# Program order on three engines in the first 18 slots of a fused attention and channel-mix kernel

## The chip, the cores and the metric

The kernel runs on one core of a Trainium2 chip. The metric is device microseconds of one execution. The core's engines run side by side and meet through semaphores: TensorE (PE in the profile, its weight loads as PEld), VectorE (DVE), ScalarE (ACT), GpSimd (POOL) and SyncE (SP), whose queue issues nearly all the transfers between HBM and the on-chip memory.

## What is computed

Biased attention over 4 batches of 8 heads, 768 positions and 64 channels a head, and behind it a channel mix with 512 channels in and 1024 hidden ones. Cut to what matters:

```python
# attention, per batch and head
scores = q @ k.T / sqrt(64) - slope[h] * dist         # kept: causal and within n_local = 96, or first n_global = 8 columns
a = exp(scores - max) / (sum + 1e-9)
x = a @ v                                             # to (batch, 768, 512)
# channel mix
xk = mu_k * x + (1 - mu_k) * x_prev                   # x_prev: the row before, zeros first
xr = mu_r * x + (1 - mu_r) * x_prev
k = maximum(xk @ w_k, 0)
out = sigmoid(xr @ w_r) * (k * k @ w_v)
```

The three weight matrices arrive as 64-bit floats (read as pairs of 32-bit words), everything else as 32-bit floats; the result is 32-bit.

## The kernel before, in words

The 3072 rows are 24 **tiles** of 128 rows, six a batch. Tiles are the steps of the main loop (line 526), and each step has four **slots**, one for each pair of heads (`hp`), so slot = 4 x step + hp. Two tiles make a **chunk** of the channel mix, 12 in all.

In a slot of an early step (0 to 8) the program traces, in this sequence: the last stage of some weights, the first stage of some weights, `transposes` for the tile of the step before, the middle stage of some weights, `scores` for this tile, `weighted` for the tile before, and then channel-mix work for 2 x 2.5 units (`run_ffn`). `scores` has the score matmuls (line 318 for the first seven tiles, in plain 32-bit; lines 320 and 321 afterwards, in split form), the bias and row maximum on VectorE (line 326) and the exponential on ScalarE (line 327), with, at the end of a tile, the reciprocals of the sums (lines 334 and 335). `transposes` turns the exponentials (line 354) and copies them out of PSUM on ScalarE (line 355). `weighted` multiplies by v (line 379), spreads the reciprocals with small matmuls (line 368), copies these on ScalarE (line 370) and, at the tile's end, forms x on VectorE (line 392).

The **weights** come as 20 blocks of 128 x 512 in four stages: `weight_load` (a 512 KB transfer), `weight_begin` (absolute value of the upper words on ScalarE, line 184, then a scaling on GpSimd, line 185), `weight_bits` (three bit operations on VectorE, lines 195 to 197, and the rounded half by ScalarE or GpSimd in turn, line 198) and `weight_end` (the rest on GpSimd, line 203). `w_pace` says how many blocks each stage should have reached at a slot: the first stage by this slot's count, the bits by that of the slot before, the end by that of two slots before, the loads five ahead. Blocks 0 to 7 are w_k, 8 to 11 w_r, 12 to 19 w_v. Raw blocks 0 to 2 and 11 to 19 lie in a pool of three buffers (`p4k`), which also holds the raw q and k from tile 8 on, the raw q of tile 7 and the mixing results; blocks 3 to 10 borrow the buffers of the first chunk. The working copies lie in a pool of four (`f2`), shared with the squared activations and the sigmoids; the middle results lie in a PSUM pool of three buffers (`ps_f`), shared with all the channel mix's matmul results.

The **channel mix** of a chunk has 40 units: 16 of kp (lines 439 to 441, then relu, square and split in lines 465 to 468 after each four), 8 of z, 16 of vps. Chunk 0 is mixed in two halves by `mix_first`, traced in slots 8 and 11, and its units start with slot 11; chunk 1 joins the queue in slot 19, with a budget of -17.5 units (line 512).

**What sets the order.** The program's trace gives each instruction a priority. A planner then lays out every engine's queue ahead of the run: it simulates a timeline and takes, on each engine, the earliest traced instruction that is ready by its own estimate, so that a queue may hold instructions in another order than traced. `keep_in_program_order` ties an instruction to the one traced before it on its engine, which fixes their sequence in the queue and adds no semaphore. The class `InOrder` wraps an engine so that its instructions are tied while `on` is true. Before the change it wraps SyncE, tied up to the end of slot 0, and ScalarE for the absolute values of blocks 0 to 7 alone. (The wrapped instructions appear under line 44.) TensorE is not wrapped.

At the start GpSimd fills with zeros the lower half of the partitions of two q buffers and two double k buffers (lines 226 and 227), 64 partitions of 1024 and 2048 elements, so that tiles with 64 channels can be multiplied as 128.

Of the kernel before, what the change touches and what calls it, by code (L numbers as in the profile page):

```python
# [9 lines left out]
F32 = mybir.dt.float32  # L10
# [4 lines left out]
AF = mybir.ActivationFunctionType  # L15
# [36 lines left out]
@with_exitstack  # L52
def tile_biased_attention_channel_mix(ctx: ExitStack, tc: tile.TileContext, qT, kT, v, n_sizes, mu_kr, w_k, w_v, w_r, q_rows, k_rows, v_rows, slopes, out):
    nc = tc.nc
    vec, act, pool, pe = nc.vector, nc.scalar, nc.gpsimd, nc.tensor
    act_in_order, sync = InOrder(tc, nc.scalar), InOrder(tc, nc.sync)

    const = ctx.enter_context(tc.tile_pool(name="const", bufs=1))

# [43 lines left out]
    zeros = const.tile([128, 512], BF16, name="zeros")  # L103
# [36 lines left out]
    for h in range(H):  # L140
        c = -8.0 * 2.0 ** -(h + 1)
# [10 lines left out]
    for h in range(H):  # L152
        c = -8.0 * 2.0 ** -(h + 1)
# [10 lines left out]
    w_raw, w_two = {}, []  # L164
# [14 lines left out]
    def weight_begin(i):  # L179

        a = f2_pool.tile([128, 512], I32, tag="f2", name=f"wa_{i}")
        (act_in_order if i < 8 else act).activation(a.bitcast(F32), w_raw[i][:, :, 1].bitcast(F32), AF.Abs, scale=2.0**111)
        pool.tensor_scalar(a.bitcast(F32), a.bitcast(F32), 2.0**-112, 2.0**-111, op0=ALU.mult, op1=ALU.mult)
        w_live[i] = a

# [12 lines left out]
    def weight_end(i):  # L200
        name, src, k, c = w_steps[i]
        hi, lo = (w[:, k, c : c + 512] for w in wts[name])
        pool.tensor_sub(lo, w_live.pop(i).bitcast(F32), hi)  # L203

    w_stages = (weight_load, weight_begin, weight_bits, weight_end)
    w_count = [0, 0, 0, 0]

    def weights_go(stage, n):
        while w_count[stage] < min(n, len(w_steps)):
            w_count[stage] += 1  # L210
            w_stages[stage](w_count[stage] - 1)
# [10 lines left out]

    qz = [q_pool.tile([128, H, 128], F32, name=f"qz_{i}", tag="qh") for i in range(2)]
    kz = [kw_pool.tile([128, 2, H, 128], F32, name=f"kz_{i}", tag="kw") for i in range(2)]
    for i in range(2):
        pool.memset(qz[i][64:128], 0.0)
        pool.memset(kz[i][64:128], 0.0)

    k_ring = [kz[0][:, 0], kz[0][:, 1], kz[1][:, 0]]
    k_glob = kz[1][:, 1, :, 0:GMAX]  # L230
# [29 lines left out]
    def load_v(n):  # L260
        b, t = divmod(n, NT)
        va = v_pool.tile([128, DM], F32, name=f"va_{n}", tag="va")
        sync.dma_start(va, v[b, t * 128 : (t + 1) * 128, :])
        state.setdefault(n, {})["va"] = va

    def global_v(n):

        b, t = divmod(n, NT)
        if t >= 2:
            sync.dma_start(state[n - 1]["va"][0:32], v[b, 0:32, :])  # L270
# [74 lines left out]
    def transposes(n, hp):  # L345
        s = state[n]
        nb = 2 if n % NT else 1
        pt = ps_t.tile([128, 512], F32, name=f"t_{n}_{hp}", tag="t")
        et = et_pool.tile([128, 512], F32, name=f"et_{n}_{hp}", tag="et")
        for u in range(2):  # L350
            e = s["e"].pop(2 * hp + u)
            for k in range(nb):
                c = (u * nb + k) * 128
                pe.transpose(pt[:, c : c + 128], e[:, k * 128 : (k + 1) * 128], ident)  # L354
        act.copy(et[:, : 2 * nb * 128], pt[:, : 2 * nb * 128])  # L355
        s["et", hp] = et

    def weighted(n, hp):
        t = n % NT
        s = state[n]  # L360
        if hp == 0:
            s["av"] = ps_a.tile([128, 512], F32, name=f"av_{n}", tag="av")
        if hp == 2 and n < EARLY:

            rb = ps_t.tile([128, 4, 128], F32, name=f"rb_{n}", tag="t")
            for h in range(H):
                a, o = divmod(h, 2)
                pe.matmul(rb[64 * o : 64 * o + 64, a, :], s["r"][:, h : h + 1].to_broadcast([128, 64]), ident, start=True, stop=True)
            s["rs"] = et_pool.tile([128, 4, 128], F32, name=f"rs_{n}", tag="et")
            act.copy(s["rs"], rb)  # L370
        et = s.pop(("et", hp))
        blocks = [state[n - 1]["va"], s["va"]] if t else [s["va"]]
        nb = len(blocks)
        for u in range(2):
            h = 2 * hp + u
            o = s["av"][64 * u : 64 * u + 64, hp * 128 : (hp + 1) * 128]
            for k, vt in enumerate(blocks):
                c = (u * nb + k) * 128
                pe.matmul(o, vt[:, h * 64 : (h + 1) * 64], et[:, c : c + 128], start=k == 0, stop=k == nb - 1)  # L379
        if hp == 3:  # L380
            c, i = divmod(n, 2)
            if i == 0:
                xt = x_pool.tile([128, 4, 257], F32, name=f"x_{c}", tag="x")
                state["x", c] = xt
                if t == 0:
                    pool.memset(xt[:, :, 0:1], 0.0)
                else:
                    pool_copy(xt[:, :, 0:1], state["x", c - 1][:, :, 256:257])
            xt = state["x", c]
            xo, av = xt[:, :, 1 + 128 * i : 129 + 128 * i], s["av"].rearrange("p (a q) -> p a q", a=4)  # L390
            if n < EARLY:
                vec.tensor_mul(xo, av, s["rs"])  # L392
            else:
                act.copy(xo, av)
# [4 lines left out]
    def mix_first(i):  # L399

        if i == 0:
            for tag in "kr":
                first_mix[tag] = [f_pool.tile([128, 4, 256], F32R, name=f"x{tag}_{p}", tag=f"x{tag}_{p}") for p in ("hi", "lo")]
        x = state["x", 0]
        c = slice(128 * i, 128 * i + 128)
        tmp = {}
        for tag in "kr":
            tmp[tag] = ps_f.tile([128, 4, 128], F32, name=f"mixp_{tag}", tag="f")
            for j in range(4):
                act.activation(tmp[tag][:, j, :], x[:, j, 128 * i : 128 * i + 128], AF.Copy, scale=mu[tag][1][:, j : j + 1])  # L410
        for tag in "kr":
            for j in range(4):
                vec.scalar_tensor_tensor(tmp[tag][:, j, :], x[:, j, 128 * i + 1 : 128 * i + 129], mu[tag][0][:, j : j + 1], tmp[tag][:, j, :], op0=ALU.mult, op1=ALU.add)
        for tag in "kr":
            act.copy(first_mix[tag][0][:, :, c], tmp[tag])
        for tag in "kr":
            vec.tensor_sub(first_mix[tag][1][:, :, c], tmp[tag], first_mix[tag][0][:, :, c])
# [80 lines left out]
    def run_ffn(amount):  # L498
        budget[0] += amount
        while budget[0] >= 1.0 and queue:  # L500
            try:
                next(queue[0])
                budget[0] -= 1.0
            except StopIteration:
                queue.pop(0)
        if not queue:
            budget[0] = 0.0

    def go_ffn(c):
        queue.append(ffn(c))  # L510
        if c == 1:
            budget[0] = -17.5

    def w_pace(slot):

        return slot + 1 if slot < 8 else 8 + (slot - 7) * 4 // 3 if slot < 11 else 12 + (slot - 10) * 8 // 5
# [9 lines left out]
    for step in range(NTILES + 1):  # L526
        for hp in range(4):
            slot = 4 * step + hp
            sync.on = slot < 1
            if step <= EARLY:  # L530
                weights_go(3, w_pace(slot - 2))
                weights_go(1, w_pace(slot))
                if step:
                    transposes(step - 1, hp)
                weights_go(2, w_pace(slot - 1))
                scores(step, hp)
                if slot == 8:
                    mix_first(0)
                if step:

                    for i in ([] if hp == 0 else [hp - 1]) + ([3] if hp == 3 else []):
                        weighted(step - 1, i)
                    if hp == 3:
                        global_v(step)
                        if step % 2 == 0:
                            go_ffn(step // 2 - 1)
            else:
                if hp == 0 and step > EARLY + 1:
                    for i in range(4):
                        weighted(step - 2, i)  # L550
                    global_v(step - 1)
                transposes(step - 1, hp)
                if step < NTILES:
                    scores(step, hp)
                if hp == 0 and step > EARLY + 1 and step % 2:
                    go_ffn((step - 3) // 2)
            run_ffn(2.5)
            run_ffn(2.5)
            if hp == 1 and step + 1 < NTILES:
                split_tile(step + 1)  # L560
            if hp == 3 and step + 2 < NTILES:
                load_tile(step + 2)
            if hp == 3 and 2 < step + 1 < NTILES:
                load_v(step + 1)
            weights_go(0, w_pace(slot) + 5)
# [171 lines left out]
```

## Time and profile before

| what | value |
|---|---|
| median of 3 runs | 527.38 us (526.9 to 528.51) |
| profiled execution | 527.59 us, its span 525.8 us |
| TensorE busy | 504.0 us, 96% of the span |
| VectorE, ScalarE, GpSimd busy | 354.7, 320.6, 240.3 us |
| instructions | 10204 |
| moved | 46.88 MB, mean 89 GB/s |

The span runs from the first to the last instruction of the profiled execution. A matmul's end is modelled in the profile, so consecutive matmuls overlap in it, and the distance between their starts tells more than their duration. In rows of the timeline the columns are the start, the time covered, the engine, the line, the operation, the tile written and those read, the shapes and the count; in square brackets stands the engine's idle time just before and what ended it. In rows of groups, the busy time and mean duration (ns) stand behind the first bar and the idle time behind the second.

### The profile page before, as it was taken

To read this page: it belongs to the slowest core of one execution; us is meant where nothing else is said; L and a number is where in the kernel's file an instruction comes from. 1 tells how busy PE (TensorE), PEld (TensorE's weight loads), DVE (VectorE), ACT (ScalarE), POOL (GpSimd) and SP (SyncE) were. 2 spreads that over 40 slices of the span, in tenths; PEclk is the share of its full clock that TensorE was granted. 3 is DMA by queue.
4 is the path that set the end of the run, shared out by engine and by line. 5 is a ranking of instruction groups with operands and counts; after the bars stand their busy time and mean duration, and the time that the engine had idled before them with its cause. 6 is when DMAs were issued, how large, how long until landed. Compare 5 with 4: busy or idle time off the path is not lost.

```text
span 525.8 us, 10204 instructions
## 1 busy us (share of the span) xinstructions
PE 504.0 (96%) x3674; PEld 441.8 (84%) x3674; DVE 354.7 (67%) x844; ACT 320.6 (61%) x738; POOL 240.3 (46%) x364
## 2 busy tenths in 40 slices
PE   7889898979999999999999999999999999999995
PEld 4678786869898898898898898898898898898984
DVE  6899878798343876766876875875886872732521
ACT  4979966436257649648558657657668658553320
POOL 8484455882103563654464653544555543412100
PEclk9999999899999999999999999999999999999998
DMA  8994435313200560440430540630620400100101
GB/s 233 345 267 108 118 70 185 81 41 98 84 20 7 151 175 1 129 123 2 140 102 1 141 113 1 160 93 2 169 72 17 130 28 14 52 6 1 41 2 45
DMA packets 19418, 46.88 MB, mean 89 GB/s; under 512 B 2976, under 2 KB 5024, under 8 KB 19360
## 3 DMA queue, kind: packets, MB, share of 16 engines
q1 hardware_dynamic: 19216, 46.15, 31.3%
q8 instruction: 31, 0.51, 0.4%
q14 instruction: 27, 0.22, 0.1%
q10 hardware_dynamic: 144, 0.00, 0.0%
HBM read 39.85 MB, written 6.29 MB: 88 GB/s over the span
## 4 chain that ended last, share of the span: by engine, by line
PE 80%; DMA 9%; DVE 5%; POOL 1%; SPq 1%; issue 1%; ACT 1%; DVEq 0%; POOLq 0%; ACTq 0%
PE kp L439 8%; PE vps L441 8%; PE vps L439 8%; PE vps L440 8%; PE kp L440 8%; PE kp L441 8%; PE av L379 7%; PE t L354 6%; PE z L439 4%; PE z L441 4%; PE z L440 4%; PE s L320 3%; PE s L321 3%; DMA kz<-in_kT_dram 2%; DMA w<-in_w_k_dram 2%; DMA w<-in_w_v_dram 2%
## 5 line engine op out<-in xcount | busy, mean ns | idle before, releaser
L343 POOL TENSOR_SCALAR e<-e,r 128x256 f32<-128x256 f32 (+1 forms) x128 | 62.3, 505 | 126.9 <-DVE r L340 104.1
L439 PE MATMUL kp<-xk_hi,wk_hi 128*128 128x256 f32 x384 | 108.7, 284 | 0.0
L440 PE MATMUL kp<-xk_lo,wk_hi 128*128 128x256 f32 x384 | 107.8, 281 | 0.0
L441 PE MATMUL kp<-xk_hi,wk_lo 128*128 128x256 f32 x384 | 107.6, 280 | 0.0
L326 DVE CUSTOM_DVE_ANT_0 e<-s,pat 128x256 f32<-128x256 f32 (+1 forms) x192 | 69.2, 396 | 55.9 <-PE s L321 45.8
L327 ACT ACTIVATE e<-e,nmax 128x256 f32<-128x256 f32 (+1 forms) x192 | 93.0, 487 | 16.8 <-DVE nmax L326 15.8
L440 PE MATMUL vps<-wv_lo,kk_hi 128*128 128x512 f32 x192 | 75.7, 394 | 1.1 <-POOL wv_lo L203 1.1
L441 PE MATMUL vps<-wv_hi,kk_lo 128*128 128x512 f32 x192 | 76.2, 397 | 0.0
L439 PE MATMUL vps<-wv_hi,kk_hi 128*128 128x512 f32 x192 | 75.6, 395 | 0.0
L439 PEld LDWEIGHTS kp<-xk_hi,wk_hi 128*128 128x128 f32 x384 | 72.5, 189 | 1.1 <-issue 0.5
L440 PEld LDWEIGHTS kp<-xk_lo,wk_hi 128*128 128x128 f32 x384 | 72.5, 189 | 0.5
L441 PEld LDWEIGHTS kp<-xk_hi,wk_lo 128*128 128x128 f32 x384 | 72.6, 189 | 0.0
L355 ACT COPY et<-t 128x512 f32<-128x512 f32 (+1 forms) x96 | 52.3, 548 | 18.8 <-PE t L354 17.2
L354 PE MATMUL t<-ident,e 128*128 128x128 f32 x352 | 56.2, 280 | 0.5 <-ACT e L327 0.3
L467 ACT CAST kk_hi<-kk 128x512 fp32r<-128x512 f32 x48 | 29.8, 620 | 43.7 <-DVE kk L466 43.6
L379 PE MATMUL av<-et,va 128*64 128x128 f32 x704 | 50.6, 280 | 3.3 <-DVE x L392 2.3
L354 PEld LDWEIGHTS t<-ident,e 128*128 128x128 f32 x352 | 41.1, 141 | 11.3 <-issue 4.3
L465 ACT ACTIVATE kk<-kp 128x512 f32<-128x512 f32 x48 | 28.5, 593 | 35.2 <-PE kp L441 34.6
L466 DVE TENSOR_TENSOR kk<-kp,kk 128x512 f32<-128x512 f32 x48 | 33.1, 690 | 24.3 <-ACT kk L465 23.5
L379 PEld LDWEIGHTS av<-et,va 128*64 128x64 f32 x704 | 40.7, 137 | 10.4 <-issue 3.3
L468 DVE TENSOR_TENSOR kk_lo<-kk,kk_hi 128x512 fp32r<-128x512 f32 x48 | 33.7, 702 | 20.6 <-ACT kk_hi L467 20.4
L440 PEld LDWEIGHTS vps<-wv_lo,kk_hi 128*128 128x128 f32 x192 | 36.1, 188 | 9.1 <-POOL wv_lo L203 1.3
(109 smaller groups left out, 1058.7 us busy)
## 6 DMA issues: line engine op xcount, KB each, us to landing
kraw<-in_kT_dram SPq DMA_DIRECT2D x36, 256.0 KB, 4.0
qraw<-in_qT_dram SPq DMA_DIRECT2D x34, 256.0 KB, 4.1
va<-in_v_dram SPq DMA_DIRECT2D x24, 256.0 KB, 3.1
out_dram<-sig SPq DMA_DIRECT2D x24, 256.0 KB, 2.0
w<-in_w_k_dram SPq DMA_DIRECT2D x8, 512.0 KB, 8.2
w<-in_w_v_dram SPq DMA_DIRECT2D x8, 512.0 KB, 3.9
w<-in_w_r_dram SPq DMA_DIRECT2D x4, 512.0 KB, 11.5
qz<-in_qT_dram SPq DMA_DIRECT2D x7, 256.0 KB, 6.1
```

Source lines behind the costliest of these rows:

```text
L326: vec.tensor_tensor_reduce(out=e[:, :w], in0=o, in1=p[:, h, :], op0=ALU.add, op1=ALU.min, scale=-0.125, scalar=3.0e38, accum_out=s["nmax"] ...
L327: act.activation(e[:, :w], e[:, :w], AF.Exp, bias=s["nmax"][:, h : h + 1], scale=-1.0, accum_out=s["sum"][:, h : h + 1])
L343: pool.tensor_scalar(e[:, :w], e[:, :w], r[:, u : u + 1], 1.0, op0=ALU.mult, op1=ALU.mult)
L354: pe.transpose(pt[:, c : c + 128], e[:, k * 128 : (k + 1) * 128], ident)
L355: act.copy(et[:, : 2 * nb * 128], pt[:, : 2 * nb * 128])
L379: pe.matmul(o, vt[:, h * 64 : (h + 1) * 64], et[:, c : c + 128], start=k == 0, stop=k == nb - 1)
L439: pe.matmul(o, sh, mh, start=first, stop=False)
L440: pe.matmul(o, sh, ml, start=False, stop=False)
L441: pe.matmul(o, sl, mh, start=False, stop=last)
L466: vec.tensor_mul(kk, pv, kk)
L467: act.copy(kkh[:, 2 * fp : 2 * fp + 2, :], kk)
L468: vec.tensor_sub(kkl[:, 2 * fp : 2 * fp + 2, :], kk, kkh[:, 2 * fp : 2 * fp + 2, :])
```

## The change

VectorE, ScalarE, GpSimd and SyncE are all wrapped. On the first three the tie is off while the constants are set up, on for slots 0 to 17 and off again from slot 18; SyncE's stays as it was. The separate wrapper for the absolute values of blocks 0 to 7 goes, as these fall into the tied slots. GpSimd zeroes only the first q buffer and the first half of the first k buffer; the rest, 64 partitions of 4096 elements in all, is written by ScalarE in eight copies of 512 elements from a tile of zeros. The text that came with the change also names a longer lag for the second chunk; the diff holds no such line, and -17.5 stands in both kernels.

```diff
-    vec, act, pool, pe = nc.vector, nc.scalar, nc.gpsimd, nc.tensor
-    act_in_order, sync = InOrder(tc, nc.scalar), InOrder(tc, nc.sync)
+    vec, act, pool, sync = (InOrder(tc, e) for e in (nc.vector, nc.scalar, nc.gpsimd, nc.sync))
+    pe = nc.tensor
+    vec.on = act.on = pool.on = False
...
-        (act_in_order if i < 8 else act).activation(a.bitcast(F32), w_raw[i][:, :, 1].bitcast(F32), AF.Abs, scale=2.0**111)
+        act.activation(a.bitcast(F32), w_raw[i][:, :, 1].bitcast(F32), AF.Abs, scale=2.0**111)
...
-    for i in range(2):
-        pool.memset(qz[i][64:128], 0.0)
-        pool.memset(kz[i][64:128], 0.0)
+    def zero(dst):
+
+        dst = dst.rearrange("p h c -> p (h c)")
+        for c in range(0, dst.shape[1], 512):
+            act.copy(dst[:, c : c + 512], zeros[64:128])
+
+    pool.memset(qz[0][64:128], 0.0)
+    pool.memset(kz[0][64:128, 0], 0.0)
+    zero(qz[1][64:128])
+    zero(kz[0][64:128, 1])
+    zero(kz[1][64:128, 0])
+    zero(kz[1][64:128, 1])
...
             sync.on = slot < 1
+            vec.on = act.on = pool.on = slot < 18
```

## The prediction

> **What bounds the kernel now.** I read the page's totals first, then the busy time by stretches, then the instruction counts of TensorE up to two moments, and last the timeline. The profiled execution took 527.59 us with a span of 525.8; the median of the runs is 527.38, so the sum below starts from 527.6 and needs no correction.
>
> ```profile
> PE 504.0 (96%) x3674; PEld 441.8 (84%) x3674; DVE 354.7 (67%) x844; ACT 320.6 (61%) x738; POOL 240.3 (46%) x364
> ```
> ```profile
> 0.00:57.00 57.00, 47.87 (x402) 39.07 (x402) 49.69 (x169) 45.95 (x139) 36.91 (x57) 1.00 0.76 220
> 57.00:117.00 60.00, 52.81 (x403) 45.04 (x401) 50.15 (x105) 34.17 (x81) 38.43 (x44) 0.97 0.40 108
> 117.00:500.00 383.00, 383.00 (x2773) 341.01 (x2774) 250.22 (x566) 236.81 (x515) 164.92 (x264) 1.00 0.26 71
> ```
>
> The columns are TensorE, weight loads, VectorE, ScalarE, GpSimd, granted clock, DMA share and GB/s. From 117 us to 500 TensorE never stops, so the end is 117 plus fixed matmul work. Nothing in the diff removes a matmul. The time can change only by what TensorE leaves unused ahead of that steady stretch. Its busy time hides part of this, since ends are modelled and overlap. I therefore count instructions and multiply by the distance between starts in dense places.
>
> ```profile
> 17.69 1.06 PE L318 MATMUL s<-kz,qz 128*128 128x128 f32 x8
> 18.68 1.09 PE L368 MATMUL rb<-ident,r 128*64 128x128 f32 x16
> 19.60 0.61 PE L379 MATMUL av<-et,va 128*64 128x128 f32 x8
> 20.14 1.32 PE L354 MATMUL t<-ident,e 128*128 128x128 f32 x8
> 24.72 0.66 PE L354 MATMUL t<-ident,e 128*128 128x128 f32 x4
> 25.21 0.61 PE L318 MATMUL s<-kz,qz 128*128 128x128 f32 x4
> 96.20 0.39 PE L439 MATMUL z<-wr_hi,xr_hi 128*128 128x512 f32 x1
> 96.44 0.40 PE L440 MATMUL z<-wr_lo,xr_hi 128*128 128x512 f32 x1
> 108.10 0.28 PE L439 MATMUL kp<-xk_hi,wk_hi 128*128 128x256 f32 x1
> 108.22 0.29 PE L440 MATMUL kp<-xk_lo,wk_hi 128*128 128x256 f32 x1
> ```
>
> Scores 0.99/8 = 0.124 us, rb 0.92/16 = 0.058, av 0.54/8 = 0.068, transposes 0.49/4 = 0.12, 512-wide z or vps 0.234, 256-wide kp 0.117. Counts up to 57 us, then up to 117:
>
> ```profile
> L318 PE MATMUL s<-kz,qz 128*128 128x128 f32 x168 | 25.4, 300 | 4.4 <-DVE nmax L326 2.6 <-DMA kz<-in_kT_dram 1.1 <-POOL wa L185 0.6
> L354 PE MATMUL t<-ident,e 128*128 128x128 f32 x56 | 9.8, 289 | 0.3 <-ACT e L327 0.3
> L379 PE MATMUL av<-et,va 128*64 128x128 f32 x104 | 9.2, 282 | 2.5 <-DVE x L392 2.3 <-DMA va<-in_v_dram 0.2
> L368 PE MATMUL rb<-ident,r 128*64 128x128 f32 x64 | 4.9, 278 | 0.7 <-DVE r L335 0.7
> ```
> ```profile
> L318 PE MATMUL s<-kz,qz 128*128 128x128 f32 x192 | 29.1, 299 | 4.7 <-DVE nmax L326 2.9 <-DMA kz<-in_kT_dram 1.1 <-POOL wa L185 0.6
> L379 PE MATMUL av<-et,va 128*64 128x128 f32 x192 | 17.0, 288 | 3.3 <-DVE x L392 2.3 <-DMA va<-in_v_dram 1.1
> L354 PE MATMUL t<-ident,e 128*128 128x128 f32 x96 | 16.0, 286 | 0.5 <-ACT e L327 0.3 <-ACT et L355 0.2
> L439 PE MATMUL kp<-xk_hi,wk_hi 128*128 128x256 f32 x40 | 11.5, 287 | 0.0
> L368 PE MATMUL rb<-ident,r 128*64 128x128 f32 x112 | 9.0, 297 | 3.4 <-ACT et L355 2.7 <-DVE r L335 0.7
> L440 PE MATMUL vps<-wv_lo,kk_hi 128*128 128x512 f32 x16 | 6.5, 405 | 1.1 <-POOL wv_lo L203 1.1
> ```
> ```profile
> 0.00:117.00 117.00, 21.13 (x64) 0.98 0.58 163
> ```
>
> The last row is line 439 alone: 64 = 40 kp + 16 vps + 8 z, and lines 440 and 441 have as many of each. By 57 us: 168 x 0.124 + 56 x 0.12 + 104 x 0.068 + 64 x 0.058 = 38.3 us of work, 18.7 unused. By 117 us the same forms give 55.0, kp 120 x 0.117 = 14.0, z and vps 72 x 0.234 = 16.8, a first few scores of tile 7 about 1: 86.8, so **30.2 unused, 18.7 of it before 57 us and 11.5 after.**
>
> **The change, part by part.** (1) Order on VectorE, ScalarE and GpSimd in slots 0 to 17. It adds no instruction. Each engine must issue what the slots trace in that sequence, so a waiting instruction holds all behind it. Counting the pace function by slot, all 20 weights must now pass before slot 18: one a slot up to slot 10, two in slot 11, then 1, 2, 1, 2, 2. Before, VectorE had converted 12 by 57 us and mixed in whatever attention was ready. Prices:
>
> ```profile
> 21.52 0.68 DVE L197 SCALAR_TENSOR_TENSOR wa<-w,wb 128x512 int32<-128x512 int32 x1
> 22.12 0.68 DVE L392 TENSOR_TENSOR x<-av,rs 128x512 f32<-128x512 f32 x1
> 30.53 0.42 DVE L326 CUSTOM_DVE_ANT_0 e<-s,pat 128x256 f32<-128x256 f32 x1
> 30.88 0.69 DVE L196 SCALAR_TENSOR_TENSOR wb<-w,wb 128x512 int32<-128x512 int32 x1
> 44.01 0.35 DVE L413 SCALAR_TENSOR_TENSOR mixp_k<-x,mus,mixp_k 128x128 f32<-128x128 f32 x1
> 44.26 0.69 DVE L195 TENSOR_SCALAR wb<-wa 128x512 int32<-128x512 int32 x1
> ```
>
> By starts, a 512-wide operation takes 0.60, so a weight 1.8 us; two score reductions of a slot 0.7 (about 0.42 in tile 0); a first-mix half 8 x 0.25 + 2 x 0.60 = 3.2. VectorE up to the end of slot 11: tile 0 with three weights 1.7 + 5.4 = 7.1; slots 4 to 7 at 2.5, 10.0; slots 8 to 11, five weights 9.0, scores 2.8, both first-mix halves 6.4; reciprocals and x products 2.0. That is 37.3 us without any wait.
>
> (2) The start. VectorE's line 148 took 1.89 us and ended with a GpSimd memset:
>
> ```profile
> 5.57 1.94 POOL L227 MEMSET kz<- 64x2048 f32 x1
> 5.69 1.89 DVE L148 TENSOR_SCALAR btmp<-btmp,sizes 128x96 f32<-128x96 f32 x1
> 9.82 0.28 DVE L326 CUSTOM_DVE_ANT_0 e<-s,pat 128x128 f32<-128x128 f32 x1
> ```
>
> The edit leaves GpSimd qz[0] and half of kz[0], done near 4 us, and gives ScalarE eight 64x512 copies. The nearest row for one is a 128x512 ScalarE copy or cast with 0.5 us between starts (82.06 to 82.56 in the rows below), so 4 us, or 2 to 5; they lie in ScalarE's idle time before 8.58 us, when its pattern products begin. Without that cover they would add those 4 us to the start. The first reduction then starts at about 7.8 instead of 9.82, a gain of 2.0 (bounds 0, if the copies delay tile 0, and 2.5). I take 2.0.
>
> (3) The waits that order adds. The first weights land late: the chain of waits holds a weight transfer of 8.93 us.
>
> ```profile
> 5.85 8.93 DMA w<-in_w_k_dram
> 82.06 0.60 ACT L467 CAST kk_hi<-kk 128x512 fp32r<-128x512 f32 x1
> 82.56 0.62 ACT L198 CAST wv_hi<-wa 128x512 fp32r<-128x512 f32 x1
> ```
> ```profile
> 86.02 0.69 DVE L197 SCALAR_TENSOR_TENSOR wa<-w,wb 128x512 int32<-128x512 int32 x1
> 86.79 0.33 SPq L44 DMA_DIRECT2D w<-in_w_v_dram  x1
> 91.36 0.67 ACT L184 ACTIVATE wa<-w 128x512 f32<-128x512 f32 x1 [0.89 <-DMA w<-in_w_v_dram]
> ```
>
> Weight 1 lands near 13 us by that duration; with ScalarE's and GpSimd's first steps its bits start at 14.3, where VectorE would have stood at 10: 4.3 us. Behind it wait the reductions of slot 2 and the exponentials on them. At each tile's end the reciprocal waits for two exponentials, 0.9 us, three times: 2.7; behind it wait the x product and the next weight. Each first-mix half chases eight ScalarE operations that start only after the exponentials, 1.25 us each: 2.5. The squaring of the first kp group in slot 11 waits for its 24 matmuls, 2.8. Sum 12.3, against nothing if all of it were hidden. Slot 12 then begins at 7.8 + 37.3 + 12.3 = **57 us** (45 with no wait). TensorE can do by then only what VectorE released: tile 0 5.0, tile 1 9.0, the scores of tile 2 4.0, one slot ahead 1.0, the first kp group 2.8: 21.8 us (a full tile: 32 scores, 16 transposes, 32 av, 16 rb). **Unused 35.2, against 18.7 before: 16.5 lost.** TensorE's own order is free, but its score buffers reach two slots and no other matmul is ready, since chunk 0 is mixed in slot 11.
>
> From there TensorE has work: slots 12 to 17 at 2.25 us of attention and 21.7 of chunk 0's 28 us, 35 together, beside 25 us of VectorE. The raw buffers of weights 14 to 19 are those of weights 11 to 16. A transfer goes out after the last bit operation, and its ScalarE step starts 5.3 us later (86.02 to 91.36). Held in sequence, weight 19 asks for it inside slot 15, and behind it on ScalarE stand a transposed copy, two weight casts, two exponentials, rs and the sigmoids, which hold two of the three feed-forward PSUM buffers. SP's queue, left free, carries these six transfers. I price what TensorE loses from 57 us on, b, at 5: one such round trip. Bounds: 0, since a third PSUM buffer and 35 us of work may cover it, and 16, three round trips in the open. After slot 17 nothing is pinned, all weights are done, and TensorE's 9 us a tile exceeds what the others need.
>
> The 11.5 us that were lost between 57 and 117 (VectorE and GpSimd converting the last eight weights while tile 7's q waits for their buffers) go. **Sum: 527.6 + 16.5 - 11.5 + 5 = 537.6, say 538.** The 2.0 of the start is inside the 7.8.
>
> On the clock, the granted value is 1.00 up to 57 us in the row above, with all the short stops there. [...]
>
> (4) The lag. The text of the change names a longer lag for chunk 1, but the diff leaves line 512 at -17.5; it costs and brings nothing.
>
> **The rivals.** *Waits hidden, faster.* Order costs only VectorE's work: slot 12 at 45 us, unused 45 - 21.8 = 23, a little b of 2 to 4, against 30.2: -5 to -3, about 523 (the end without any b is 520.4). For it: the 11.5 us after 57 go for certain, and the late weights of before are the reason for them. Against it: a reciprocal cannot start before its exponentials, and VectorE was already busy 49.69 of the first 57 us, so a wait there is not refilled. *Nothing moves*: half of the 12.3 hidden and b near 2 gives 23 + 6 + 2 - 30.2 = 0.8 us, about 528. *The round trips in the open, slower still*: weights 15, 17 and 19 each hold ScalarE for the 5.3 us; b = 16 gives 549. For it: there is no earlier free buffer; against it: the two weights of a slot leave VectorE and TensorE other work meanwhile. *The order is not what it says*: unpinned work of slots 18 and on may be drawn ahead into the gaps. Ten exponential buffers and two score buffers let that be one slot, 2 us of TensorE; 536, inside the forecast.
>
> **How the numbers follow.** A measurement here can tell about 0.3%, 1.6 us, from no change. Forecast (with the fourth rival) 0.56, open round trips 0.12, together slower 0.68; nothing moves 0.10; waits hidden 0.22. The predicted time is 538, its own range 530 to 549. The full range takes in the zero-wait end in part, 521 to 549.
>
> **What would show it.** Right: 12 weights done and the first kp matmul near 50 to 57 us; TensorE idle behind reductions (line 326) before slot 12; sigmoids held behind a weight activation (line 184) that waits for DMA; the last weight's bits near 85 to 90 us, not 107; steady TensorE from about 95 us. The start: first reduction before 8 us and line 148 under 0.5. Wrong: slot 12 reached before 48 us, or TensorE's instruction count by 57 us close to 402, or the steady stretch beginning with less than 30 us unused.

## The result and the profile after

The changed kernel takes 557.41 us (median of four runs, 557.07 to 558.39), the kernel before 527.14 us beside it (526.02 to 528.51): a ratio of 1.055, 95% interval 1.051 to 1.060. Slower by 30 us, where the prediction said 10 and ended its range at 549. The direction was right, the size was not.

The page's totals and its row of granted clock, in 40 slices of 13.9 us:

```profile
span 556.6 us, 10211 instructions
PE 516.6 (93%) x3674; PEld 450.4 (81%) x3674; DVE 357.2 (64%) x844; ACT 329.7 (59%) x748; POOL 232.0 (42%) x362
PEclk7576698799999999999999999999999999999999
```

TensorE executes as many matmuls as before. The busy times by stretches (TensorE, weight loads, VectorE, ScalarE, GpSimd, granted clock, DMA share, GB/s):

```profile
0.00:57.00 57.00, 37.34 (x198) 27.95 (x198) 42.16 (x126) 35.76 (x96) 31.14 (x50) 0.67 0.62 189
57.00:117.00 60.00, 45.56 (x284) 39.07 (x285) 32.27 (x69) 27.56 (x60) 20.50 (x25) 0.83 0.23 73
117.00:500.00 383.00, 383.00 (x2893) 340.12 (x2893) 265.04 (x626) 251.82 (x572) 175.91 (x280) 1.00 0.30 80
```

By 57 us TensorE has done 198 matmuls where before it had done 402, and in the next 60 us 284 instead of 403. VectorE, tied, does 126 and 69 operations where it did 169 and 105. From 117 us on TensorE never stops, as before, so everything is decided by then. The groups of TensorE up to 57 us, then its larger ones up to 72.5 us:

```profile
L328 PE MATMUL s<-kz,qz 128*128 128x128 f32 x80 | 18.7, 412 | 10.0 <-DVE nmax L44 6.6 <-DMA kz<-in_kT_dram 2.0 <-POOL kz L44 1.4
L364 PE MATMUL t<-ident,e 128*128 128x128 f32 x28 | 7.1, 372 | 1.3 <-ACT rs L44 1.3
L389 PE MATMUL av<-et,va 128*64 128x128 f32 x48 | 5.9, 380 | 6.3 <-ACT et L44 6.3
L378 PE MATMUL rb<-ident,r 128*64 128x128 f32 x32 | 3.1, 353 | 0.4 <-ACT et L44 0.4
```
```profile
L364 PE MATMUL t<-ident,e 128*128 128x128 f32 x32 | 7.8, 361 | 3.3 <-ACT rs L44 3.3
L449 PE MATMUL kp<-xk_hi,wk_hi 128*128 128x256 f32 x17 | 6.0, 353 | 4.0 <-ACT xk_hi L44 4.0
```

With the prediction's distances between starts, work by 57 us is 80 x 0.124 + 28 x 0.12 + 48 x 0.068 + 32 x 0.058 = 18.4, so 38.6 us are unused; by 72.5 us, four more transposes and 49 kp matmuls (17 and twice 16) make 24.6, 47.9 unused. The same count gives 60.6 at 117 us and 61.1 at 150 us, against 30.2 and 32.0 before. The difference at the end, 29.1, is the measured 30: the accounting holds, and two of its entries were wrong. In the order of time:

**The start.** VectorE's rows, after:

```profile
4.64 0.66 DVE L44 TENSOR_SCALAR btmp<-btmp,sizes 128x128 f32<-128x128 f32 x3
7.62 0.29 DVE L44 CUSTOM_DVE_ANT_0 e<-s,pat 128x128 f32<-128x128 f32 x1 [0.18 <-PE s L328]
10.31 0.69 DVE L44 TENSOR_SCALAR wb<-wa 128x512 int32<-128x512 int32 x1 [1.94 <-POOL wa L44]
12.38 0.28 DVE L44 CUSTOM_DVE_ANT_0 e<-s,pat 128x128 f32<-128x128 f32 x1
```

The first reduction starts at 7.62 us instead of 9.82. But the second slot's reduction stands behind the first weight's bits, which wait for the transfer and its first two steps, and starts at 12.38. Before, the plan put all eight reductions of tile 0 ahead of the first weight:

```profile
9.82 0.28 DVE L326 CUSTOM_DVE_ANT_0 e<-s,pat 128x128 f32<-128x128 f32 x1
12.81 0.29 DVE L326 CUSTOM_DVE_ANT_0 e<-s,pat 128x128 f32<-128x128 f32 x1
16.43 0.69 DVE L195 TENSOR_SCALAR wb<-wa 128x512 int32<-128x512 int32 x1
```

**Slots 8 to 11.** VectorE, GpSimd and TensorE, rows of the timeline of after:

```profile
34.18 0.68 DVE L44 TENSOR_SCALAR wb<-wa 128x512 int32<-128x512 int32 x1
34.90 0.70 DVE L44 SCALAR_TENSOR_TENSOR wb<-w,wb 128x512 int32<-128x512 int32 x1
35.63 0.69 DVE L44 SCALAR_TENSOR_TENSOR wa<-w,wb 128x512 int32<-128x512 int32 x1
39.55 0.42 DVE L44 CUSTOM_DVE_ANT_0 e<-s,pat 128x256 f32<-128x256 f32 x1 [3.23 <-PE s L328]
42.61 1.53 DVE L44 SCALAR_TENSOR_TENSOR mixp_k<-x,mus,mixp_k 128x128 f32<-128x128 f32 x4 [2.28 <-ACT mixp_k L44]
46.90 0.68 DVE L44 TENSOR_SCALAR wb<-wa 128x512 int32<-128x512 int32 x1
52.39 0.69 DVE L44 TENSOR_SCALAR wb<-wa 128x512 int32<-128x512 int32 x1
60.99 1.53 DVE L44 SCALAR_TENSOR_TENSOR mixp_k<-x,mus,mixp_k 128x128 f32<-128x128 f32 x4 [1.65 <-ACT mixp_k L44]
70.48 0.69 DVE L44 TENSOR_TENSOR kk<-kp,kk 128x512 f32<-128x512 f32 x1 [5.12 <-ACT kk L44]
71.86 0.69 DVE L44 TENSOR_TENSOR kk_lo<-kk,kk_hi 128x512 fp32r<-128x512 f32 x1 [0.69 <-ACT kk_hi L44]
72.47 0.69 DVE L44 TENSOR_SCALAR wb<-wa 128x512 int32<-128x512 int32 x1
```
```profile
36.40 0.62 POOL L44 TENSOR_SCALAR wk_hi<-wa 128x512 fp32r<-128x512 f32 x1 [1.77 <-DVE wa L44]
36.98 0.40 POOL L44 TENSOR_SCALAR kz<-kz 64x256 f32<-64x256 f32 x1
```
```profile
37.43 5.15 PE L328 MATMUL s<-kz,qz 128*128 128x128 f32 x24 [1.44 <-POOL kz L44]
63.19 0.58 PE L449 MATMUL kp<-xk_hi,wk_hi 128*128 128x256 f32 x1 [3.97 <-ACT xk_hi L44]
```

The first weight bits of a slot mark its beginning: slot 8 at 34.18, slot 9 at 46.90, slot 11 at 52.39, slot 12 at 72.47 us, not 57. Unused TensorE time, counted as above, is 24.3 us when slot 8 begins and 36.4 when slot 11 does. In slot 8 a circle closes that the prediction did not see: GpSimd's rounding of a weight waits for VectorE's bits, GpSimd's copy of the global columns of k for tile 2 stands behind it, the scores wait for that copy, and VectorE waits 3.23 us for the scores.

**Behind slot 12.** ScalarE, TensorE and VectorE, after:

```profile
101.25 0.66 ACT L44 ACTIVATE wa<-w 128x512 f32<-128x512 f32 x1 [4.93 <-DMA w<-in_w_v_dram]
```
```profile
98.01 0.79 PE L449 MATMUL z<-wr_hi,xr_hi 128*128 128x512 f32 x1 [4.77 <-DVE wa L44]
98.60 0.63 PE L450 MATMUL z<-wr_lo,xr_hi 128*128 128x512 f32 x1
99.03 0.63 PE L451 MATMUL z<-wr_hi,xr_lo 128*128 128x512 f32 x1
```
```profile
97.27 0.69 DVE L44 SCALAR_TENSOR_TENSOR wa<-w,wb 128x512 int32<-128x512 int32 x1
111.22 0.69 DVE L44 SCALAR_TENSOR_TENSOR wa<-w,wb 128x512 int32<-128x512 int32 x1
116.57 0.42 DVE L44 CUSTOM_DVE_ANT_0 e<-s,pat 128x256 f32<-128x256 f32 x1 [4.66 <-PE s L328]
```

ScalarE waits 4.93 us for one transfer into a raw buffer, up to 101.25. TensorE's own stop comes before that: 4.77 us up to 98.01, when VectorE's third bit operation of a weight, begun at 97.27, is done. By the kernel's pools that operation is the last reader of a buffer of the PSUM pool from which z's buffer comes too. While ScalarE waits, TensorE has z's matmuls, 0.43 us apart at a granted clock of 0.50, instead of 0.234 at 1.00 (89.0 to 91.5 us). By count the stop loses 4.8 us (52.8 unused at 93.2, 57.6 at 98.0), z's matmuls behind it 2.2 (59.8 at 103), and everything from there to 117 us 0.8. The last weight's bits end at 111.9 us.

### The profile page after: what moved, and what is told of

Read it like the earlier page. It is cut to its first block, busy times and chain, and to the rows that moved or that the text cites. A ratio compares the mean times of both kernels' runs of the same rounds, so it can differ in the third digit from the quotient of the medians.

```text
span 556.6 us, 10211 instructions
## 1 busy us (share of the span) xinstructions
PE 516.6 (93%) x3674; PEld 450.4 (81%) x3674; DVE 357.2 (64%) x844; ACT 329.7 (59%) x748; POOL 232.0 (42%) x362
## 5 line engine op out<-in xcount | busy, mean ns | idle before, releaser
L449 PE MATMUL kp<-xk_hi,wk_hi 128*128 128x256 f32 x384 | 110.1, 288 | 4.4 <-ACT xk_hi L44 4.0
L450 PE MATMUL kp<-xk_lo,wk_hi 128*128 128x256 f32 x384 | 109.2, 285 | 0.9 <-DVE xk_lo L44 0.9
L451 PE MATMUL kp<-xk_hi,wk_lo 128*128 128x256 f32 x384 | 108.9, 284 | 0.0
L449 PEld LDWEIGHTS kp<-xk_hi,wk_hi 128*128 128x128 f32 x384 | 73.9, 193 | 6.1 <-ACT xk_hi L44 4.2
L450 PEld LDWEIGHTS kp<-xk_lo,wk_hi 128*128 128x128 f32 x384 | 73.9, 192 | 1.7 <-DVE xk_lo L44 1.2
L451 PEld LDWEIGHTS kp<-xk_hi,wk_lo 128*128 128x128 f32 x384 | 73.9, 193 | 0.2 <-issue 0.2
L364 PE MATMUL t<-ident,e 128*128 128x128 f32 x352 | 57.5, 283 | 3.3 <-ACT rs L44 3.3
L44 ACT ACT_TABLE_LOAD x40 | 51.3, 1283 | 13.9 <-PE z L451 9.7
L449 PE MATMUL z<-wr_hi,xr_hi 128*128 128x512 f32 x96 | 40.0, 416 | 4.8 <-DVE wa L44 4.8
```

Source lines behind the costliest of these rows:

```text
L44: ins = f(*args, **kwargs)
L449: pe.matmul(o, sh, mh, start=first, stop=False)
L450: pe.matmul(o, sh, ml, start=False, stop=False)
L451: pe.matmul(o, sl, mh, start=False, stop=last)
```

## The experiments

Each kernel was run beside the kernel before. The zeros alone were run twelve times, the others once each, and one run tells no better than some 3 us: of the 17 runs of the kernel before beside the zeros, 16 lie between 524.85 and 531.10 us. "Unused" is the prediction's measure, at 57, 72.5 and 117 us.

**Which edit: the zeros or the order.**

```diff
# zeros alone, on the kernel before
-    for i in range(2): pool.memset(qz[i][64:128], 0.0); pool.memset(kz[i][64:128], 0.0)
+    (the changed kernel's zero() and its six lines)
# order alone, on the changed kernel: these lines put back
+    for i in range(2): pool.memset(qz[i][64:128], 0.0); pool.memset(kz[i][64:128], 0.0)
```

> The kernel before with the zero padding of the later buffers alone moved to ScalarE, no order tied. The forecast's part (2) by itself: the first reduction starts near 7.6 us instead of 9.82, and if that start is worth its 2 us at the end, 525.1; if the transfers of the first weights and tiles set the pace after it, 527 (no change). Tied order as the only cause of the loss expects no slower than 527.

> The changed kernel with the zero padding back on GpSimd as before, the three engines tied in slots 0 to 17. If order is the whole loss: 557 plus the 2 us that the start gained, 557 to 560. If the ScalarE copies or the new start had a hand in it: clearly under 555.

The zeros alone: 529.92 us against 527.6, ratio 1.005 (1.002 to 1.008); neither 525.1 nor 527, so the expected gain is not there, rather a small loss. The order alone: 556.01 us, 28.4 above. That is 1 us under the forecast for order as the whole loss, and within what one run tells it is the whole change. That the first reduction comes early is true of the zeros too. Rows of VectorE and of TensorE's waits up to 57 us, zeros alone:

```profile
7.49 0.29 DVE L336 CUSTOM_DVE_ANT_0 e<-s,pat 128x128 f32<-128x128 f32 x1
```
```profile
PE s L328 <- POOL wa L185: 3.4, 1, 3.4
```

The first reduction is 2.3 us earlier and 22.2 us are unused by 57 us, against 18.7. With nothing tied, the planner laid out other queues: TensorE's differ from the first score groups on, and scores stand 3.4 us behind a weight's scaling on GpSimd (0.6 before). But by 117 us little of this is left (31.2 unused against 30.2), and by 150 us the distance is 3.9 again (35.9 against 32.0). So this wait is not shown to be the loss, whose cause stays open.

**Which engine's order.** Each with the wrapper of the first eight absolute values as in the kernel before, except the last:

```diff
-            vec.on = act.on = pool.on = slot < 18
+            vec.on = slot < 18        # or act.on alone, or pool.on alone, or vec.on = act.on
```

> The changed kernel with VectorE alone tied in slots 0 to 17 (ScalarE only for the absolute values of blocks 0 to 7, as before). VectorE converts the weights in sequence and is the fullest engine up to 57 us. Theory of VectorE's waits: most of the 30 us, 545 to 557. Theory that the loss needs engines that wait for each other in turn: under 540.

> The changed kernel with ScalarE alone tied in slots 0 to 17. ScalarE's weight activations wait for raw buffers and hold exponentials behind them. Theory of VectorE's waits: under 535. Theory that ScalarE's waits for weight transfers and for the mixing carry it: 540 to 550. Engines waiting for each other in turn: under 540, as for VectorE alone.

> The changed kernel with GpSimd alone tied in slots 0 to 17. GpSimd's copies of the global columns (k) stood behind a weight copy in the changed kernel and held the scores of tile 2 from 34 to 39.5 us. Theory that GpSimd's order matters by itself: 532 to 540. Theory of VectorE's waits, or of engines waiting in turn: within 2 us of 527.

> The changed kernel with GpSimd left free and VectorE and ScalarE tied in slots 0 to 17. GpSimd alone cost 9 us, VectorE alone 22, ScalarE alone 8, all three 30. If what GpSimd's order costs is inside what VectorE's costs: 549 to 557. If it adds to it: 545 or less.

VectorE alone 549.51 us (22 above the kernel before), ScalarE alone 535.26 (8), GpSimd alone 536.17 (9), VectorE and ScalarE 556.5 (28). VectorE's order is most of it, as the theory of its waits said; ScalarE's 535.26 is at the edge of that theory's forecast (under 535) and below the one for its own waits (540 to 550). The two add up, 22 and 8 to 28, within what one run tells. GpSimd's order costs 9 alone, as the theory of its own order said, and nothing clear on top of the other two. Alone, its cost is in one group of matmuls, over the whole run (4.7 us of idle time in the kernel before):

```profile
L329 PE MATMUL s<-kz,qz 128*128 128x128 f32 x192 | 30.7, 314 | 13.2 <-POOL kz L44 11.3
```

The longest of these stops, 8.8 us, is the wait of tile 2's scores for GpSimd's copy. With GpSimd left free and the other two tied, the 3.23 us of slot 8 are gone, but slot 8 begins 1.5 us later (35.67); slot 12 begins 1.5 us earlier (70.98), and the end comes 0.9 earlier.

**The clock.** Is the granted 0.67 a cause? Six 128x512 matmuls on zeros ahead of each slot's scores in slots 0 to 17, and 16 ahead of the first kp, fill TensorE's idle time:

```diff
+        for _ in range(6 if 4 * n + hp < 18 else 0):
+            pe.matmul(ps, zeros[:, 0:128], zeros, start=True, stop=True)
```

> The changed kernel with six extra 128x512 bf16 matmuls of zeros into the score buffer ahead of each slot's scores in slots 0 to 17, and sixteen ahead of the first kp group; their results are overwritten. They fill TensorE's stops, so the granted clock (0.50 to 0.71 from 8 to 72 us) should rise. Theory of the slow clock: score groups of 8 take 1.06 us and not 2.05, the first kp group 2.8 and not 5.8, and the time falls by 8 to 15, to 543 to 549. Theory of tied waits alone: 555 to 560, the clock being a consequence.

555.63 us, and slot 12 begins 2.7 us earlier. The stretches, and VectorE's wait for the first square:

```profile
0.00:57.00 57.00, 44.20 (x276) 27.57 (x277) 42.43 (x127) 36.39 (x98) 31.69 (x51) 0.94 0.63 190
57.00:117.00 60.00, 53.63 (x346) 41.55 (x345) 33.46 (x73) 29.49 (x67) 19.83 (x24) 0.97 0.22 73
```
```profile
67.77 0.69 DVE L44 TENSOR_TENSOR kk<-kp,kk 128x512 f32<-128x512 f32 x1 [3.00 <-ACT kk L44]
```

The clock is back at 0.94 and 0.97 (0.67 and 0.83 in the change), VectorE waits 3.00 us for the first square instead of 5.12, and VectorE still does 127 operations by 57 us. This is the forecast of tied waits. The low clock of the change went with TensorE's waiting (38.6 us unused in the first 57); given back, it brings 1.8 us of 30, which one run hardly tells from nothing (the added matmuls may have eaten a part).

**Which work held in sequence.** The changed kernel with a part left free: all weight steps; weights 12 to 19 alone; the mixing of `mix_first` and all operations of the channel mix; these two together. Here a tie links an instruction to the last tied one of its engine, so that one left free can be put anywhere. This tie with nothing left free was not run; with the late weights free, unused time is the change's up to 57 us.

```diff
-            if self.on:
-                self.tc.keep_in_program_order(ins)
+            if self.on and not self.free:
+                (tie ins to self.last, the last tied one)
...
+        vec.free = act.free = pool.free = w_count[stage] > 0      # > 12: the late weights alone
...
+                    loose(True)                                   # around mix_first, go_ffn and run_ffn
```

> The changed kernel with all weight conversions left free and everything else in slots 0 to 17 tied to one another, so that weights may fill the waits. Theory that the loss comes from weights standing in sequence with attention: 525 to 533, near the time before. Theory that attention and mixing in their traced order wait for each other anyway: 540 to 557.

> The changed kernel with weights 12 to 19 free and everything else in slots 0 to 17 tied to one another. These are the weights whose raw buffers come round late; ScalarE waited for their transfers 0.3, 0.5 and 4.9 us, and from 72.5 to 119 us TensorE left 12.7 us unused. Theory that their place in the sequence makes that loss: 557 less 8 to 13, 544 to 549. Theory that the loss sits in slots 0 to 11 (unused 47.9 us by 72.5 against 20.9 before) and stays: 552 to 557.

> The changed kernel with the first mixing of slots 8 and 11 and all channel-mix work free, attention and weights in slots 0 to 17 tied to one another. VectorE stood 2.3, 1.7 and 5.1 us at the mixing and at the first square. Theory that weights and attention in sequence carry the loss: 548 to 557. Theory that the mixing in sequence carries it, since the next weights stand behind it: 533 to 545.

> The changed kernel with the first mixing, the channel mix's operations and weights 12 to 19 free, the rest tied in slots 0 to 17. Alone, the one was worth 15 us (542) and the other 11 (546). Theory A, two different waits (the mixing in slots 8 and 11 ahead of slot 12; the buffers' round trips behind it): they add up, 557 - 26 = 531, between 529 and 535, and unused TensorE time at 117 us near 36. Theory B, one chain of waits seen from two ends: together not more than the larger one, 540 to 543.

| left free | us | above the kernel before beside it | unused at 57, 72.5, 117 us |
|---|---|---|---|
| nothing (the change) | 557.41 | 30 | 38.6, 47.9, 60.6 |
| all weights | 536.51 | 9 | 35.2, 36.1, 39.1 |
| late weights | 546.25 | 18 | 38.6, 45.1, 48.3 |
| mixing and channel mix | 542.17 | 13 | 38.1, 41.4, 44.1 |
| late weights, mixing and channel mix | 540.54 | 14 | 36.1, 37.4, 43.2 |

Against 557.41 us all weights were worth 21, which lies between the forecasts, the late weights 11, the mixing 15, and these two together 17 and not 26, as the theory of one chain seen from two ends said. That the late weights are late because they stand behind slot 11's mixing and square fits this; with the mixing free they are hardly in the way. VectorE with the mixing free:

```profile
36.39 0.36 DVE L43 SCALAR_TENSOR_TENSOR mixp_k<-x,mus,mixp_k 128x128 f32<-128x128 f32 x1 [0.19 <-ACT mixp_k L43]
36.69 0.36 DVE L43 SCALAR_TENSOR_TENSOR mixp_r<-x,mus,mixp_r 128x128 f32<-128x128 f32 x1
36.95 0.35 DVE L43 SCALAR_TENSOR_TENSOR mixp_k<-x,mus,mixp_k 128x128 f32<-128x128 f32 x1
39.59 0.41 DVE L43 CUSTOM_DVE_ANT_0 e<-s,pat 128x256 f32<-128x256 f32 x1
```

The mixing now fills the 3.23 us in which VectorE waited for tile 2's scores; the reduction starts at 39.59, in the change at 39.55.

**Which slots.** The tie ends with slot 7, or with slot 11:

```diff
-            vec.on = act.on = pool.on = slot < 18
+            vec.on = act.on = pool.on = slot < 8         # or slot < 12
```

> The changed kernel with the three engines tied in slots 0 to 7 only, ahead of the first mixing. By the changed kernel's trace slot 8 starts at 34 us with TensorE's unused time near 24 us, against 15 before at 31. Theory that a loss made there stays: 535 to 540. Theory that free order behind it makes it good, since TensorE lacks no work before 57 us that it could not do later: 525 to 531.

> The changed kernel with the three engines tied in slots 0 to 11 only. In the changed kernel TensorE's unused time was 47.9 us at the end of slot 11 (72.5 us) against 20.9 before at the same moment, and 61 against 32 at the end. Theory that the loss is made in slots 0 to 11: 545 to 557. Theory that it is made by the raw-buffer round trips of slots 12 to 17: 527 to 540.

> The same kernel as the one tied in slots 0 to 11 that took 2760 us, once more. If that time belongs to the program, it comes again within a per cent, with about 1.04 us from one matmul to the next. If it belonged to that execution, the time is one of these: loss made ahead of slot 12 (theory A) 545 to 550, since slots 0 to 7 cost 5 us and slots 8 to 11 some 13 to 18 more; loss made behind slot 12 (theory B) 535 or less.

Slots 0 to 7: 533.28 us, 5 above the kernel before and between the two forecasts. Slots 0 to 11: in the first execution 2760.74 us, and in the second, of the same program, 539.33, 13 above. A group of kp matmuls in the one and in the other:

```profile
L449 PE MATMUL kp<-xk_hi,wk_hi 128*128 128x256 f32 x384 | 401.2, 1046 | 0.0
```
```profile
L449 PE MATMUL kp<-xk_hi,wk_hi 128*128 128x256 f32 x384 | 108.7, 284 | 0.0
```

So 2760 us belonged to that execution, not to the program (the second was on another chip; other kernels took their usual times on the first). Its 512-wide matmuls started 1.28 us apart instead of 0.234, TensorE was busy 100% of the time, and the granted clock read 1.00; VectorE, ScalarE and GpSimd were busy 345.2, 342.0 and 223.5 us in all, in the second run 346.2, 324.3 and 232.6 up to 500 us of its 537. Why is not known.

The second run shows where the loss is decided. Up to 57.2 us VectorE's timeline is the change's, within 0.03 us. Then, with slots 12 and on free (the stretch, and VectorE's rows):

```profile
57.00:117.00 60.00, 59.12 (x466) 50.47 (x465) 48.90 (x117) 43.75 (x105) 27.60 (x37) 1.00 0.44 121
```
```profile
57.52 0.42 DVE L44 CUSTOM_DVE_ANT_0 e<-s,pat 128x256 f32<-128x256 f32 x1
62.77 0.42 DVE L44 CUSTOM_DVE_ANT_0 e<-s,pat 128x256 f32<-128x256 f32 x1 [1.63 <-PE s L328]
64.08 1.14 DVE L44 SCALAR_TENSOR_TENSOR mixp_k<-x,mus,mixp_k 128x128 f32<-128x128 f32 x3 [0.53 <-ACT mixp_k L44]
```

Between 57 and 64 us VectorE does the reductions of later slots where it had stood waiting for the first mixing, TensorE is busy from there on, and 38.9 us are unused at 72.5 us and 41.9 at 117 (37.7 at 57, so 4 more; the change 22 more). It fits neither forecast, 545 to 550 for a loss made ahead of slot 12 or below 535 for one made behind it: the first 57 us lose 19 us against the kernel before (37.7 to 18.7), of which 7 come back, since the kernel before loses 11.5 in the 60 us after. Tied slots 12 to 17 turn 13 us into 30, and not only behind slot 12: of the change's 47.9 us unused at 72.5, 9.0 go when those slots' reductions may fill the waits of slot 11.

No kernel of these beats the kernel before.

## Why the prediction was right in direction and too small

**What bounds the kernel, and the measure: right.** Unused TensorE time ahead of the steady stretch gives 29 of the 30 us. The sum 527.6 + 16.5 - 11.5 + 5 had 40.2 unused in all; it is 60.6 at 117 us.

**The start, 7.8 us and "a gain of 2.0": the time right, the gain not there.** The first reduction came at 7.62 us, and the eight copies lay in ScalarE's idle time as said (2.47 to 6.71 us). The 2.0 was inside the 7.8, so slot 12's sum is right in that; but the early start bought nothing in either kernel. In the change the second slot waits for a weight until 12.38; alone, the zeros change the queues that the planner lays out, and what is lost there is open.

**The step that failed first: "Sum 12.3", the waits ahead of slot 12.** Slot 12 began at 72.5 us, not 57, with 47.9 unused instead of 35.2: 12.7 of the 20 us that were missed. By stages, from the prediction's terms and the rows above: slot 8 should have begun at 7.8 + 7.1 + 10.0 + 4.3, two reciprocals (1.8) and two thirds of the 2.0, that is 32.3, and began at 34.2; slots 8 to 10 were to take 5.4 + 2.1 + 3.2 + 1.25 = 12.0 and took 18.2; slot 11 was to take the rest, 13, and took 20.1. The waits that the sum did list for the weights and reciprocals came near: 1.94 and 1.13 us for the first two weights against 4.3, and 0.74, 0.88 and 0.81 against 0.9 at each tile's end. What it missed:

- *A wait that no term held*: tile 2's scores behind GpSimd's weight step, 3.23 us. The prediction followed VectorE's queue and did not follow GpSimd's, which was tied as well. (In the run with GpSimd free this wait is gone, and slot 12 begins 1.5 us earlier.)
- *The first-mix halves at 1.25 us of waiting each*: 2.28 and 1.65 us.
- *Operations in sequence cost more here than the same ones mixed with others.* A weight was priced at 3 x 0.60, the distance that its bits had in the kernel before beside bits of other weights (19.73, 20.33, 20.93, 21.52); tied, its bits start at 34.18, 34.90, 35.63, with the steps 0.72 and 0.73 where the next reads what the one before wrote. A weight so takes 2.05 instead of 1.8, some 3 us over twelve weights. Four mixing operations in a row, each on another quarter of the same tile, take 1.50 us, from 42.61 to 44.11, so 0.375 each; where they alternate between two tiles, in the run with the mixing free, they start 0.30 apart once and then 0.26, near the 0.25 of the price. A first-mix half takes 4.3 instead of 3.2. In these rows the distance goes by whether the next operation uses the tile that the one before wrote; why is not shown.
- *The squaring of the first kp group, 2.8*: 5.12 us, of which the run with the filled idle time shows 2.1 to be the clock; and the square and its split, 2.0 us on VectorE up to 72.47, stood in no term.

These are VectorE's account. For TensorE the tie on slots 12 to 17 adds to it: in the run tied to slot 11, where those slots' reductions may pass these waits, 9.0 of the 47.9 us are not lost.

**The step that failed second: "I price what TensorE loses from 57 us on, b, at 5."** It is 60.6 - 47.9 = 12.7 by 117 us, inside the bounds of 0 to 16, but not by the round trip that it was put on. The round trip was found, with its place and near its length: one wait of 4.93 us on ScalarE, from 96.3 to 101.25, where the estimate from rows was 5.3. But 9.7 of the 12.7 were lost by 98.0 us, 4.8 of them in the stop that ended with VectorE's bits, and from 98 on TensorE had z's matmuls. ScalarE's waits for these transfers hardly changed either, while b did. From 72.5 to 119 us they are 5.7 us in the change, 3.9 in the kernel before, 4.9 with the mixing free and 3.3 with the late weights free; b is 12.7 in the change, 2.7 with the mixing free (44.1 - 41.4) and 3.2 with the late weights free (48.3 - 45.1). The stop of 4.77 us for a weight's bits is 0.9 with the mixing free and absent with the late weights free. So by these rows b holds in the main TensorE's wait for VectorE's queue, in which weights, squares and reductions stand in sequence, and the slower z matmuls behind that wait. The prediction had called those slots well supplied ("TensorE has work").

**"The 11.5 us ... go": borne out where it can be seen.** In the run tied to slot 11 only 4 are lost after 57 us. In the change itself 22 are lost there, and nothing separates them.

**The clock.** The prediction's sum did without it, on a granted 1.00. In the change 0.67 was granted in the first 57 us and 0.83 in the next 60, where the kernel before had 1.00 and 0.97. At the stop of 4.77 us, TensorE fell idle at 93.2 and began again at 98.0; the granted clock was 1.00 up to 96.5, 0.50 from 96.7 to 103.5 and 1.00 from 103.6 on. In size the clock is a small term: 2.1 us at the first kp group by the rows, 2.2 at z's matmuls, and 1.8 at the end by the run with filled idle time.

**The lag.** The same constant stood in both kernels and cost nothing, as said.

**The rivals.** *Waits hidden* and *nothing moves* fell with slot 12 at 72.5. *The round trips in the open* had the sign, but put three of them at 16 us; one was open, TensorE had work beside it, and 57.6 of the 60.6 us unused lay ahead of 98 us. *The order is not what it says* fell; these are the groups of VectorE's reductions up to 111.9 us, after:

```profile
L44 DVE CUSTOM_DVE_ANT_0 e<-s,pat 128x256 f32<-128x256 f32 x24 | 9.1, 418 | 6.1 <-PE s L328 6.1
L44 DVE CUSTOM_DVE_ANT_0 e<-s,pat 128x128 f32<-128x128 f32 x8 | 2.0, 284 | 0.2 <-PE s L328 0.2
```

When the last weight is done, 32 reductions are through, those of 16 slots at two each: nothing of slot 18 and on was drawn ahead.

Of the signs named ahead, the idle behind reductions (6.6 us by 57) and behind a weight activation waiting for a transfer were seen, and the early first reduction. The first kp matmul at 63.2 us instead of 50 to 57, the last bits at 111.9 instead of 85 to 90, and a steady TensorE from about 110 instead of 95 said that the size was wrong.

## What to carry to other kernels

An order fixed on several engines is priced as a chain across all of them: follow each wait to the engine that ends it, and see what stands ahead there, not only in the queue that you cost. Their separate removals need not add up (15 and 11 us gave 17 together; the 3.23 us of slot 8 brought 1.5 at slot 12), because other waits of the sequence take the place of the one removed. A long wait on one engine is not yet a loss: ask what the engine that bounds the kernel does meanwhile (4.93 us on ScalarE stood beside z's matmuls). And take the durations of operations on one tile from rows in which they stand next to each other.

## What the runs showed of the hardware beside it

VectorE's 512-wide integer operations started 0.60 us apart in the kernel before, where neighbours worked on different tiles (19.73 to 21.52 us), and 0.72 and 0.73 in the change, where each read what the one before wrote (34.18 to 35.63). 128-wide mixing operations that alternated between two tiles started 0.26 apart in the run with the mixing free (36.69 to 36.95), and four in a row on one tile took 1.50 in the change (42.61 to 44.11). A granted clock of 0.67 in a stretch with 38.6 of 57 us unused went to 0.94 with matmuls of zeros in the gaps, and the time fell by 1.8 us in one run. One execution of a program that takes 539 us took 2760 instead, with 512-wide matmuls 1.28 us apart (516.07, 517.35, 518.63 us) instead of 0.234 at a granted clock shown as 1.00; whether that can be seen coming is open.
